# Talking-heads attention and a squared-ReLU layer on one core: the planner's DMA constants and TensorE's order replaced

## The chip, the cores and the metric

The kernel runs on one core of a Trainium2 chip. Its engines work side by side and wait for each other by semaphores: TensorE (PE, with its weight loads as PEld), VectorE (DVE), ScalarE (ACT), GpSimd (POOL) and SyncE (SP). DMA transfers are issued by POOL (queue q0) and SP (queue q1) and share 16 DMA engines. The metric is the device time of one execution in microseconds, the median of several runs.

## The reference

```python
# q, k, v: (8, 12, 448, 64); w_pre, w_post: (12, 12)
scores = scale * np.matmul(q, k.transpose(0, 1, 3, 2))
scores = np.einsum('bhij,hg->bgij', scores, w_pre)
scores = scores - np.max(scores, axis=-1, keepdims=True)
attn = np.exp(scores)
attn = attn / (np.sum(attn, axis=-1, keepdims=True) + 1e-09)
attn = np.einsum('bhij,hg->bgij', attn, w_post)
attn_out = np.matmul(attn, v)
x = attn_out.transpose(0, 2, 1, 3).reshape(3584, 768)
h = np.maximum(x @ w_in, 0.0)          # w_in (768, 2048)
out = h * h @ w_out                    # w_out (2048, 768)
```

The heads are mixed by a 12 x 12 matrix before the softmax and by another one after it.

## The kernel before

Each of the eight batches goes through the same steps, and the steps of several batches are interleaved. A step is cut into units of TensorE; a unit is a few matmuls into one or two of the eight PSUM banks, followed by evictions on ACT or DVE.

- Transposes (`emit_T`, matmuls on line 726) turn q and k into `qkt`.
- QK units (`emit_QK`, L879) multiply a tile of up to 128 query rows with all keys, for one pair of heads; the result is evicted into `stage` (L486 on ACT, L487 on DVE). `stage` holds three such tiles (NSG = 3). A unit is written as two matmuls of 128 columns, or as four of 64 where `QK_QUAD` has a "1".
- Relayouts (`emit_rel`, L925): a DMA issued by SP moves ten query rows of all 12 heads, a chunk of 105 KB, from `stage` to one of 16 slots of `dring`, where the heads lie along the partitions. A relayout waits for all evictions of its tile and for the pre unit that last read its slot.
- Pre units (`emit_pre`, L948) mix the heads of a pair of chunks; they are the only readers of `dring`. ACT takes the exponential with row sums (L965), DVE the reciprocal (L979), POOL scales the second mixing matrix (L986) and a part of the exponentials (L1001).
- The first 22 chunks of batch 0 go another way: direct units (`emit_direct`, L824) multiply with q already scaled by the mixing weights, with no relayout. The scaled q lies in the space of `w_out_sb` and `h2t` until then.
- Post units (`emit_post`, L1036 and L1050) mix the heads after the softmax and transpose on the way; their results go to `a2t` (L486, L487). AV units (`emit_AV`, L1120) multiply with v.
- First-layer units (`emit_F1`, L1176 in full tiles, L1184 in half-row tiles) and second-layer units (`emit_F2`, L1303 or L1311; L1251 for the last two tiles) are the two matrix products behind attention. ReLU is taken at the eviction (L1213, L1214), the square on DVE (L1223).
- Filler matmuls (L599) keep TensorE's array busy in the first 60 us where the planner sees a gap.

Loads of q, k, v and of both weight matrices and the stores of the output are issued by POOL. In the first 60 us that includes both weight matrices, eight loads of 384 KB each.

Nothing of the order is written out by hand except TensorE's. `_Plan.run` plays the whole program through with a cost for each task. TensorE takes its units from ten streams (transposes 0, QK 1, pre 2, post 3, AV 4, direct 5, first layer 6 and 7, second layer 8 and 9), and `ORDER` is the string that says which stream is next; within a stream units keep their order. Every other task is placed on its engine when the plan finds it ready, and evictions (`FLEX`) go to ACT or DVE, whichever the plan expects to end them earlier. So the constants of the plan and `ORDER` set the order on every engine; the waits between engines are real semaphores.

For DMAs the plan keeps two queues, "move" (relayouts) and "load" (everything else). In `dma_next` a transfer that is alone goes at full rate, and where both queues move at once each goes at a part of it. `_finish` adds `MARGIN` to the time at which a task that waits for a DMA may start, by the DMA's kind and the waiting engine: the first number up to 110 us, the second behind it.

Of the kernel before, what the change touches and what calls it, by code (L numbers as in the profile page):

```python
# [10 lines left out]
PE = "pe"  # L11
# [4 lines left out]
FLEX = "flex"  # L16
# [7 lines left out]
DMA_AHEAD = 3900.0  # L24
DMA_SLOW = {"move": 1.0, "load": 1.04}
DMA_END = {"move": 3700.0, "load": 2300.0}
MARGIN = {("move", PE): (1200.0, 700.0), ("move", FLEX): (1900.0, 1600.0),
          ("load", PE): (0.0, 900.0)}
INF = float("inf")
ORDER = (  # L30
    "0010555105055105515555551155311555513005555555315555135500155555531355331552200355511155"
    "1123333242234421126631731367227322776333631627613167122244413176313762122777623376633366"
    "2127776201902938338392281938020224441223663200811181118333813277116621277133626613377132"
    "2441141337721267612667322001667722383383338226771020283167202760238113813183138314212442"
    "2229391119333933922291444229119316116337221763363372217601026713722633602027237318302028"
    "1181118322911931393139312422442218113813381138322444221636372127633637212763362002277200"
    "2611637337339202091229119118133813181318222444223933191139331922244422818138333836212672"
    "2176336020167137336222772200637316722009119131922393831383118311822244422183138313822444"
    "2286113617137336221673373621167200227633713702206228318338382002911192229391393319222931"
    "9383138111811381224442244422367116317373337226666221763733637212791229833839228833932244"  # L40
    "42228823238687666733633637777866444776676668678676787977788999898999"
)
F1_FULL = "1111111111111111111111111111111100000000000001000000010000000110001010001111011111111111"
F2_FULL = "00000000000000000000000000101100"
QK_QUAD = "000000000001000000000000000000000000000000001000000000000000001000000000000000000000000000000000000000000000000000000000000000000000000000000000000000000000000"
POST_QUAD = "0000000000000000000000000000000000000000000000000000000000000000000000000000000000000000000000000000000000000000000000000000000000000000000000000000000000000000000000000000000001100000"


# [57 lines left out]
class _Plan:  # L106
# [89 lines left out]
    def _finish(self, t):  # L196
        t.done = True
        for s in t.succs:
            s.nwait -= 1
            spare = MARGIN.get((t.dma[0], s.engine), (0.0, 0.0)) if t.dma else (0.0, 0.0)  # L200
            s.avail = max(s.avail, t.end + SEM_LAT + spare[0 if t.end < 110e3 else 1])
# [14 lines left out]
    def dma_next(self, go=False):  # L216

        a = self.moving["move"][0] if self.moving["move"] else None
        b = self.moving["load"][0] if self.moving["load"] else None
        if a is None and b is None:  # L220
            return INF
        now = self.moved
        left = [a[1] if a else 0.0, b[1] if b else 0.0]
        while True:
            on = [x is not None and x[0] <= now for x in (a, b)]
            then = min([x[0] for x in (a, b) if x is not None and x[0] > now] + [INF])
            if not any(on):
                now = then
                continue
            rate = (1.0, 1.0)  # L230
            if all(on):
                rate = (0.22, 0.52)
                if b[2] <= 200.0:
                    rate = (47.8 / (54.0 + b[2]), 0.72)
            end = [now + left[i] / rate[i] if on[i] else INF for i in range(2)]
            first = min(end)
            to = min(first, then)
            for i in range(2):
                if on[i]:
                    left[i] -= (to - now) * rate[i]  # L240
            now = to
            if first <= then:
                x = (a, b)[end.index(first)]
                break
        if go:
            self.moved = now
            for i, y in enumerate((a, b)):
                if y is not None:
                    y[1] = left[i]
            t = x[3]  # L250
            self.moving[t.dma[0]].pop(0)
            t.end = max(t.end, now + DMA_END[t.dma[0]]
                        + (1800.0 if t.dma[0] == "load" and 20e3 < now < 45e3 else 0.0))
            self._finish(t)
        return now
# [96 lines left out]
def bass_talking_heads_attention__then__ffn_squared_relu_kernel(  # L352
# [45 lines left out]
    with ExitStack() as es:  # L398
# [460 lines left out]
        def emit_QK(b, T):  # L859
# [8 lines left out]
            for p in ((0, 3, 1, 4, 2, 5) if n == 0 else range(0, NP, IT // w)):  # L868
                g = _Group(2)

                quad = w == PJ or QK_QUAD[len(qk_units)] == "1"

# [608 lines left out]
```

## Time and profile before

| | |
|---|---|
| median of 3 runs | 521.75 us (521.67 to 521.86) |
| profiled execution | 521.25 us |
| its span, first to last instruction | 519.5 us |
| mean granted TensorE clock | 0.997 |
| busy: PE, PEld, DVE, ACT, POOL | 507.5, 320.9, 402.2, 434.2, 267.3 us |
| DMA moved | 72.32 MB, mean 139 GB/s |
| relayouts' queue q1 / loads' and stores' queue q0 | 36.86 MB / 33.83 MB |

The span is cut into windows by time: for each one the busy time of the engines, the clock that TensorE was granted (1.00 is full speed) and the busy share of the DMA engines are listed. A chain of waits follows the program back from its last instruction, at each step to what released it. In the timeline, numbers in brackets are the idle time of an engine before an instruction and what ended it. Ends of matmuls are modelled, and matmuls overlap, so how long a unit takes is read from the start of one unit to the start of the next.

### The profile page before, as it was taken

The page shows a single profiled execution, that of the slowest core. Times are in us where ns is not written, and L with a number is a line of the kernel's source. Part 1 is how long each engine was busy: PE and PEld are TensorE (multiplying, and loading weights), DVE is VectorE, ACT ScalarE, POOL GpSimd, SP SyncE. Part 2 cuts the span into 40 slices and gives each one's busy share as a digit, 9 for nine tenths or more (in the row PEclk, how much of TensorE's full clock was granted, in tenths as well). Part 3 has the DMA queues.
Part 4 walks back from the last instruction along what each step waited for, and adds up shares of the span by engine and source line. Part 5 has one row for each costly group of instructions (what it writes and reads, how often), then busy time and mean ns, then how long its engine had stood idle before and what let it go on. Part 6 is the DMA issues. An engine that isn't in the chain of part 4 may idle for free.

```text
span 519.5 us, 22375 instructions
## 1 busy us (share of the span) xinstructions
PE 507.5 (98%) x9163; PEld 320.9 (62%) x9163; DVE 402.2 (77%) x1032; ACT 434.2 (84%) x1249; POOL 267.3 (51%) x571
## 2 busy tenths in 40 slices
PE   7999998999999999999999999999999999999997
PEld 3455776667776664566556665566555665568874
DVE  8998997689988859879998879887897677855220
ACT  4989997889999988988889888888988887878531
POOL 9936665452674486434963459235664444343000
PEclk9999998999999999999999999999999999999999
DMA  8999999834896589746993679736994367551013
GB/s 114 193 229 183 217 173 185 179 101 105 151 190 149 132 174 186 153 92 151 176 182 71 144 161 188 159 86 139 171 174 107 89 142 144 106 117 33 3 34 88
DMA packets 83021, 72.32 MB, mean 139 GB/s; under 512 B 7160, under 2 KB 80424, under 8 KB 82920
## 3 DMA queue, kind: packets, MB, share of 16 engines
q0 software_dynamic: 37632, 33.83, 40.0%
q1 hardware_dynamic: 45000, 36.86, 29.0%
q8 instruction: 74, 1.21, 0.9%
q14 instruction: 27, 0.22, 0.1%
q10 hardware_dynamic: 288, 0.20, 0.1%
HBM read 47.27 MB, written 11.01 MB: 112 GB/s over the span
## 4 chain that ended last, share of the span: by engine, by line
PE 81%; ACT 7%; DVE 6%; DMA 3%; POOL 1%; issue 1%; SPq 0%; DVEq 0%; POOLq 0%
PE ps L1311 23%; PE ps L1184 12%; PE ps L1176 11%; PE ps L948 7%; PE ps L1120 6%; PE ps L1036 5%; PE ps L879 5%; PE ps L824 4%; ACT pring L965 3%; PE ps L1303 3%; DMA dring<-stage 2%; PE ps L1251 2%; DVE stage L487 2%; PE ps L726 2%; DVE a2t L487 2%; ACT stage L486 1%
## 5 line engine op out<-in xcount | busy, mean ns | idle before, releaser
L965 ACT ACTIVATE pring<-ps 128x448 bf16<-128x448 f32 x360 | 191.8, 560 | 11.8 <-PE ps L948 9.9
L986 POOL TENSOR_TENSOR wk2s<-wk2b,rinv 128x120 bf16<-128x120 bf16 (+1 forms) x179 | 71.4, 399 | 145.5 <-DVE rinv L979 144.0
L1311 PE MATMUL ps<-w_out_sb,h2t 64*128 64x384 bf16 x1472 | 134.7, 323 | 0.2 <-ACT pring L965 0.2
L487 DVE CAST a2t<-ps 128x420 bf16<-128x420 f32 (+1 forms) x205 | 123.1, 643 | 14.6 <-PE ps L1050 14.3
L487 DVE CAST stage<-ps 128x448 bf16<-128x448 f32 (+1 forms) x178 | 107.0, 616 | 10.9 <-PE ps L879 9.2
L486 ACT ACTIVATE stage<-ps 128x448 bf16<-128x448 f32 (+1 forms) x182 | 94.8, 555 | 14.8 <-PE ps L879 13.8
L486 ACT ACTIVATE a2t<-ps 128x420 bf16<-128x420 f32 (+1 forms) x163 | 96.4, 647 | 10.9 <-PE ps L1050 10.6
L1311 PEld LDWEIGHTS ps<-w_out_sb,h2t 64*128 64x128 bf16 x1472 | 68.0, 94 | 45.0 <-issue 2.6
L1184 PE MATMUL ps<-xt,w_in_sb 64*128 64x448 bf16 (+1 forms) x840 | 88.3, 347 | 0.2
L1348 POOL DMA_DIRECT2D out_dram<-osb x52 | 33.5, 650 | 95.6 <-ACT osb L486 33.7
L965 ACT ACTIVATION_READ_ACCUMULATOR pring<-ps 128x1 f32 x360 | 80.7, 224 | 0.0
L1176 PE MATMUL ps<-xt,w_in_sb 128*128 128x228 bf16 (+2 forms) x636 | 76.6, 273 | 0.0
L1223 DVE TENSOR_TENSOR h2t<-h1t 128x448 bf16<-128x448 bf16 (+2 forms) x176 | 56.1, 343 | 22.1 <-ACT h1t L1213 19.8
L1001 POOL TENSOR_TENSOR ptail<-pring,rinv 128x128 bf16<-128x128 bf16 x171 | 70.1, 410 | 0.0
L1176 PEld LDWEIGHTS ps<-xt,w_in_sb 128*128 128x128 bf16 x636 | 59.0, 99 | 13.8 <-ACT pring L965 1.8
L1036 PEld LDWEIGHTS ps<-wk2s,pring 60*128 60x128 bf16 (+1 forms) x2184 | 48.8, 94 | 23.7 <-ACT pring L965 2.4
L1213 ACT ACTIVATE h1t<-ps 128x448 bf16<-128x448 f32 (+2 forms) x104 | 44.3, 439 | 18.7 <-PE ps L1176 8.7
L948 PE MATMUL ps<-dring,wk 64*64 64x448 bf16 (+1 forms) x676 | 54.4, 364 | 3.4 <-DMA dring<-stage 1.9
L1184 PEld LDWEIGHTS ps<-xt,w_in_sb 64*128 64x128 bf16 x840 | 37.3, 94 | 32.8 <-PE ps L879 1.4
L1036 PE MATMUL ps<-wk2s,pring 60*128 60x60 bf16 (+1 forms) x2184 | 55.5, 187 | 1.2 <-issue 0.5
L979 DVE RECIPROCAL rinv<-rowsum 128x2 f32<-128x2 f32 (+1 forms) x184 | 29.0, 158 | 31.2 <-ACT pring L965 30.3
L879 PE MATMUL ps<-qkt 64*128 64x448 bf16 (+1 forms) x366 | 50.7, 353 | 0.5 <-DVE qkt L487 0.3
(62 smaller groups left out, 562.3 us busy)
## 6 DMA issues: line engine op xcount, KB each, us to landing
dring<-stage SPq DMA_DIRECT2D x309, 105.0 KB
out_dram<-osb POOLq DMA_DIRECT2D x52, 192.0 KB, 3.8
vraw<-in_v_dram POOLq DMA_DIRECT2D x48, 128.0 KB
qraw<-in_q_dram POOLq DMA_DIRECT2D x48, 112.0 KB, 4.5
kraw<-in_k_dram POOLq DMA_DIRECT2D x48, 112.0 KB, 5.4
w_in_sb<-in_moe_w_in_dram POOLq DMA_DIRECT2D x8, 384.0 KB, 17.1
w_out_sb<-in_moe_w_out_dram POOLq DMA_DIRECT2D x8, 384.0 KB, 16.2
dring<-stage SPq DMA_DIRECT2D x30, 42.0 KB
```

Of the source, the lines that this page charges most:

```text
L486: return eng.activation(o, i_, AF.Copy)
L487: return eng.tensor_copy(o, i_)
L879: r_ = eng.matmul(ps[y * v:(y + 1) * v, g.banks[x], 0:S], qkt[r0:r0 + 64, pp, 0, j0:j0 + v], qkt[r0:r0 + 64, pp, 1 + pb, :], start=True, s ...
L948: r_ = eng.matmul(ps[64 * y:64 * y + 64, gr.banks[x], 0:S], wk1[64 * x:64 * x + 64 - R0 * x, :], dring[64 * x:64 * x + 64 - R0 * x, (g0 + ...
L965: return eng.activation(pring[:, pr, 0:S], ps[:, gr.banks[x], 0:S], AF.Exp, accum_out=rowsum[:, pr, :])
L986: return eng.tensor_tensor(wk2s[:, p0:p0 + n, :], i0.to_broadcast([128, n, PR]), rinv[:, p0:p0 + n, :].to_broadcast([128, n, PR]), ALU.mult)
L1001: return eng.tensor_tensor(ptail[:, p0 // 2, :, :], pring[:, p0:p0 + 2, 0:PJ], rinv[:, p0:p0 + 2, :].to_broadcast([128, 2, PJ]), ALU.mult)
L1036: r_ = eng.matmul(ps[z * v:(z + 1) * v, gr.banks[x], o0:o0 + PR], pring[64 * x:64 * x + PR, pr + y, c:c + v], wk2s[64 * x:64 * x + PR, pr ...
L1176: r_ = eng.matmul(ps[:, gs[ph].banks[0], 0:n], w_in_sb[:, ft, t * 128:(t + 1) * 128], xt[:, ft, c0:c1], start=(ft == 0), stop=(ft == NFT - 1))
L1184: r_ = eng.matmul(ps[:, gs[0].banks[x], 0:n], w_in_sb[64 * y:64 * y + 64, ft, t * 128:(t + 1) * 128], xt[64 * y:64 * y + 64, ft, c0:c1], s ...
L1223: return eng.tensor_tensor(h2t[:, t16, o0:o0 + n], h1t[:, s, 0:n], h1t[:, s, 0:n], ALU.mult)
L1311: r_ = eng.matmul(ps[:, gs[0].banks[hh], 0:FH], h2t[64 * y:64 * y + 64, t16, col:col + 128], w_out_sb[64 * y:64 * y + 64, t16, hh * FH:(hh ...
```

## The change

Three things are replaced: the rates at which a relayout and a load move when both are under way, which now come from a table by the load's kind (97 the first weight matrix, 79 the second, 88 q and k, 60 v, 250 the output, 54 the last output pieces); the margins; and the two strings that set TensorE's order and the form of its QK units. No unit is added or removed. `F1_FULL`, `F2_FULL` and `POST_QUAD` stay.

```diff
-MARGIN = {("move", PE): (1200.0, 700.0), ("move", FLEX): (1900.0, 1600.0),
+DMA_SHARE = {97.0: (0.295, 0.75), 79.0: (0.325, 0.74), 88.0: (0.3, 0.76),
+             60.0: (0.39, 0.76), 250.0: (0.22, 0.52), 54.0: (0.44, 0.72)}
+MARGIN = {("move", PE): (0.0, 700.0), ("move", FLEX): (700.0, 1500.0),
           ("load", PE): (0.0, 900.0)}
 ORDER = (
-    "0010555105055105515555551155311555513005555555315555135500155555531355331552200355511155"
+    "0010155055051505511551555115555113553155550033555555550105555555311553332550220555315551"
...
-QK_QUAD = "000000000001000000000000000000000000000000001000000000000000001000000000000000000000000000000000000000000000000000000000000000000000000000000000000000000000000"
+QK_QUAD = "001000000001000000000000000000000000000000001001000000010000001000000000000000000000000000000000000000000000000000000000000000000000000000000000000000000000000"
...
             rate = (1.0, 1.0)
             if all(on):
-                rate = (0.22, 0.52)
-                if b[2] <= 200.0:
-                    rate = (47.8 / (54.0 + b[2]), 0.72)
+                rate = DMA_SHARE[b[2]]
```

All eleven rows of `ORDER` change; one is shown. By the formula that goes, the first rate was 0.317 for the first weight matrix (now 0.295), 0.359 for the second (0.325), 0.337 for q and k (0.3) and 0.419 for v (0.39). For a relayout the plan's margin up to 110 us falls from 1200 to 0 ns where TensorE waits for it and from 1900 to 700 ns where an eviction does.

More of the change, by code (lines that the diff above doesn't have):

```diff
@@ L30 @@
 ORDER = (
-    "0010555105055105515555551155311555513005555555315555135500155555531355331552200355511155"
[L32 to L41, printed above, removed]
+    "0010155055051505511551555115555113553155550033555555550105555555311553332550220555315551"
+    "2313332431244123622317667223677313361372267113667313242244137611376713127721266676623336"
+    "7277128310028323839139229839200223444132622008111811181338317222167663123776313673132621"
+    "4431411367217127766327621002677622383383338162267720028332677102208311813181338314212442"
+    "2229391139313933922291444229119116316337221763363372217620016733722631620027137383200281"
+    "1181118222939133911393124222441183138311831382224442216363372217633637212763362002277200"
+    "2611637337339200292219119118131813183318222444223931193139331922244422881383138336221672"
+    "1276200167337136336222772002736316720209119313922193831183138113822244422381381338224442"
+    "2816336117117336221673373621167200226731362002713783382228382002911392219139393319222931"
+    "9318338111811382224444442236171163377331722166662227637336372127922198338392298333832244"
+    "42228876323267886673363363676787774448687787766676697767689989889999"
 )
```

## The prediction

> **What bounds the kernel now.** First the page's busy shares, then the waits of TensorE, then its busy time by windows.
>
> ```profile
> PE 507.5 (98%) x9163; PEld 320.9 (62%) x9163; DVE 402.2 (77%) x1032; ACT 434.2 (84%) x1249; POOL 267.3 (51%) x571
> PE ps L948 <- DMA dring<-stage: 1.9, 1, 1.9
> PE ps L599 <- DVE osb L584: 1.5, 1, 1.5
> PE ps L1036 <- issue: 0.5, 1, 0.5
> ```
>
> TensorE is busy for 507.5 of 519.5 us, so 12 us are all that a new order of the same work can win from idle time, and 1.5 us of them lie before the first filler matmul, where the order does nothing. The longest single wait in the program is one: a pre unit (line 948) waited 1.9 us for a relayout, the DMA from `stage` to `dring`. The windows show where that is and what follows it (columns: sum, then busy time of PE, PEld, DVE, ACT, POOL, then granted clock, DMA share, GB/s).
>
> ```profile
> 40.00:60.00 20.00, 19.10 (x359) 11.74 (x356) 18.26 (x49) 19.78 (x65) 14.06 (x30) 1.00 1.07 192
> 60.00:76.00 16.00, 15.49 (x290) 12.12 (x290) 14.71 (x48) 15.92 (x49) 8.84 (x21) 1.00 1.00 185
> 78.00:80.00 2.00, 0.38 (x4) 0.16 (x4) 0.80 (x3) 1.35 (x6) 0.92 (x3) 0.87 1.15 199
> 80.00:82.00 2.00, 2.00 (x14) 1.50 (x11) 0.47 (x2) 1.16 (x4) 0.00 (x0) 0.50 1.04 193
> 82.00:84.00 2.00, 2.00 (x20) 1.63 (x17) 1.67 (x6) 0.36 (x1) 1.29 (x3) 0.78 0.78 153
> 160.00:500.00 340.00, 338.93 (x6309) 210.97 (x6297) 261.85 (x645) 290.03 (x835) 166.47 (x365) 1.00 0.62 129
> ```
>
> From 160 to 500 us TensorE idles 1.1 us in all: nothing is to be won there. Around 79 us it idles for most of a window, and afterwards its granted clock is 0.50 and 0.78 for two windows. The chain of waits through this place:
>
> ```profile
> 54.23 1.24 PE ps L1176 x12
> 60.88 1.80 PE ps L1176 x18
> 68.17 11.36 DMA dring<-stage
> 79.53 0.09 issue
> 79.62 0.59 PE ps L948 x4
> 80.21 3.76 PE ps L1176 x24
> ```
>
> The relayout is issued at 68.17 and lands at 79.53; the pre unit starts at 79.62. A first-layer unit is six matmuls of L1176: 1.24/2 = 0.62 us at full clock. The four units after the wait took 3.76 us and not 4 x 0.62 = 2.48: the slow clock cost 1.28 us. So this one place costs 1.9 + 1.3 = 3.2 us.
>
> Why is the relayout late? The relayouts' own DMA queue (q1) in the windows 20 to 40, 40 to 60, 60 to 80 and 80 to 100 us, against the pre matmuls of the same windows (four to a pair of chunks, so to two relayouts):
>
> ```profile
> dring<-stage SPq DMA_DIRECT2D x16, 105.0 KB
> ...
> q1 hardware_dynamic: 1510, 1.25, 24.1%
> ...
> q1 hardware_dynamic: 1763, 1.46, 28.2%
> ...
> q1 hardware_dynamic: 1883, 1.56, 30.4%
> ...
> q1 hardware_dynamic: 2477, 2.05, 36.2%
> ...
> 20.00:40.00 20.00, 0.00 (x0) 0.00 (x0) 1.00 1.26 222
> 40.00:60.00 20.00, 3.25 (x40) 0.99 (x40) 1.00 1.07 192
> 60.00:80.00 20.00, 2.86 (x34) 0.98 (x34) 0.99 1.03 189
> 80.00:100.00 20.00, 2.10 (x24) 0.62 (x20) 0.93 0.96 186
> ```
>
> At 105 KB (0.1075 MB) each, 11.6, 13.6, 14.5 and 19.1 relayouts are moved, while TensorE uses 0, 20, 17 and at most 12. The stock is 11.6, then 5.2, then 2.7, then about 10. The DMA engines are full (share about 1), shared with the loads of the weights, so relayouts come at a fixed rate, TensorE takes them faster, and the stock is down to what is still in flight just before 80 us. This stage is bound by relayout traffic at that point; the rest of the program is bound by TensorE's own work.
>
> **The change part by part.** It adds no work: the same 952 TensorE units run in another order. On TensorE, at the place of the wait (L948 pre, L879 QK, L1176 first layer, L1036 and L1050 post), before:
>
> ```order
> L1176 MATMUL ps<-xt,w_in_sb 128x228 x12
> L948 MATMUL ps<-dring,wk 64x448 x4
> L879 MATMUL ps<-qkt 64x448 x4
> L948 MATMUL ps<-dring,wk 64x448 x8
> L1176 MATMUL ps<-xt,w_in_sb 128x228 x24
> L948 MATMUL ps<-dring,wk 64x448 x4
> ```
>
> The unit that waits is the second half of the x8 row; the x24 behind it are the four slow units. TensorE, the same place in the change:
>
> ```order
> L1176 MATMUL ps<-xt,w_in_sb 128x228 x18
> L879 MATMUL ps<-qkt 128x448 x2
> L1036 MATMUL ps<-wk2s,pring 128x60 x12
> L1050 MATMUL ps<-wk2b,ptail 128x60 x2
> L879 MATMUL ps<-qkt 128x448 x2
> L948 MATMUL ps<-dring,wk 64x448 x4
> L1176 MATMUL ps<-xt,w_in_sb 128x228 x12
> L948 MATMUL ps<-dring,wk 64x448 x4
> L879 MATMUL ps<-qkt 64x448 x4
> L948 MATMUL ps<-dring,wk 64x448 x4
> L1176 MATMUL ps<-xt,w_in_sb 128x228 x36
> L948 MATMUL ps<-dring,wk 64x448 x4
> ```
>
> The unit that waited is now the third row of L948. Counted over the whole program, all units that stood ahead of it still do, and four more: three first-layer units (of those that ran slow) and one post unit.
>
> Step 1, the wait. Eighteen L1176 matmuls take 1.80 us (row above). A post unit:
>
> ```profile
> 60.01 0.34 PE L1036 MATMUL ps<-wk2s,pring 60*128 60x60 bf16 x12
> 60.19 0.19 PE L1050 MATMUL ps<-wk2b,ptail 60*128 60x60 bf16 x2
> 60.31 0.57 PE L948 MATMUL ps<-dring,wk 64*64 64x448 bf16 x6
> ```
>
> From its start to the next unit's it takes 60.31 - 60.01 = 0.30 us. Together 2.10 us are put ahead. Where TensorE stopped, at 79.62 - 1.91 = 77.7 us, it now has work until 79.8, and the relayout lands at 79.53 if it lands as before. The wait of 1.9 us is covered, with 0.3 us to spare: -1.9.
>
> Step 2, the clock. Without a stop the slow clock after it goes too: -1.3. The 0.5 us stop for "issue" left the clock of its window at 1.00, so short stops do not bring it on.
>
> Step 3, other pre units. Some come earlier against their relayouts: the margins that the planner kept at first for a relayout that TensorE waits for are now zero. No row shows those waits, so I bound them: below 0, above 1.9 us, the largest wait of this kind in the trace. Since the spare above is only 0.3 us and the stock is as thin for the pairs just ahead of it, I take +0.3, nearer to zero because one such wait is all that the present order has.
>
> Step 4, evictions. The units put ahead bring three eviction-and-square pairs and two post evictions forward, into windows where ACT is busy for 19.78 of 20 and 15.92 of 16 us. They do not stand between TensorE and the pre unit except through a PSUM bank. ACT and DVE idle in the stop and behind it (windows 78 to 84 above: 3.1 of 6 us for ACT), and that takes them up: 0. If they did hold a bank, the price is one eviction, about 0.6 us.
>
> Step 5, QK units in four matmuls for two. `QK_QUAD` sets six flags in place of three, so there are three more of them:
>
> ```profile
> 74.92 0.35 PE L879 MATMUL ps<-qkt 64*128 64x448 bf16 x2
> 76.89 0.38 PE L879 MATMUL ps<-qkt 64*64 64x448 bf16 x4
> 149.51 1.30 PE ps L1311 x16
> 156.58 1.41 PE ps L1311 x16
> ```
>
> Each costs 0.38 - 0.35 = 0.03 us more, 0.09 in all, and may save a change of the array's tiling, worth 0.11 us (the second-layer unit with and without one). Counted in both orders, such changes are 261 before and 260 now. Sum 0.0.
>
> Step 6, the rest of the order, which is swapped locally. From 160 to 500 us TensorE idles 1.1 us (row above), so at most that is won, and about as much may be lost: 0.
>
> Sum for the profiled execution: 521.25 (519.5 of span and 1.75 around it) - 1.9 - 1.3 + 0.3 = 518.35. The median of the runs is 521.75, 0.5 more, so the forecast is **518.9 us**, 0.55% faster.
>
> **The rivals.** (a) The wait moves but stays. Relayouts come at a fixed rate, so a TensorE that is 3.2 us ahead may run dry at a later pair and give all of it back: 521.7 us. Against it: from 80 to 100 us 19 relayouts land and 12 are used, so the stock grows there. For it: the spare of 0.3 us, which a slightly slower relayout uses up.
>
> (b) Slower. The relayouts of the third tile of query rows (the first of batch 1) wait for that tile's last QK unit. TensorE before, with its last QK units in the x6 and in half of the x4:
>
> ```order
> L879 MATMUL ps<-qkt 128x448 x6
> L824 MATMUL ps<-qkt,h2t 128x448 x6
> L879 MATMUL ps<-qkt 128x448 x4
> L948 MATMUL ps<-dring,wk 64x448 x4
> L1036 MATMUL ps<-wk2s,pring 128x60 x12
> ```
>
> and in the change, where the last of them is the L879 row:
>
> ```order
> L948 MATMUL ps<-dring,wk 64x448 x4
> L1120 MATMUL ps<-a2t,vraw 64x220 x6
> L1120 MATMUL ps<-a2t,vraw 64x110 x4
> L1120 MATMUL ps<-a2t,vraw 64x220 x6
> L1120 MATMUL ps<-a2t,vraw 64x110 x4
> L1036 MATMUL ps<-wk2s,pring 128x60 x12
> L1050 MATMUL ps<-wk2b,ptail 128x60 x2
> L879 MATMUL ps<-qkt 128x448 x2
> L948 MATMUL ps<-dring,wk 64x448 x4
> ```
>
> Three pre units, five post units, a filler and an AV unit now stand ahead of it.
>
> ```profile
> 47.21 0.55 PE L599 MATMUL ps<-osb 128*128 128x448 bf16 x2
> 48.09 0.34 PE L1036 MATMUL ps<-wk2s,pring 60*128 60x60 bf16 x12 [0.34 <-POOL ptail L1001]
> 48.30 0.33 PE L1036 MATMUL ps<-wk2s,pring 60*128 60x60 bf16 x12
> 50.50 0.57 PE L948 MATMUL ps<-dring,wk 64*64 64x448 bf16 x8
> 47.83 4.74 SPq L925 DMA_DIRECT2D dring<-stage  x5
> 51.38 1.65 PE ps L1120 x40
> ```
>
> That is 8 x 0.21 (48.30 - 48.09) + 0.88 (48.09 - 47.21) + 0.83 (half of 1.65) = 3.4 us more TensorE work ahead of it. If SP's queue runs out of relayouts there, every later pair lands up to 3.4 us later: 79.53 becomes 82.9, TensorE is there at 79.8 and stops for 3.1 us. With the clock loss scaled to it, 1.3 x 3.1/1.9 = 2.1, the sum is 518.05 + 3.1 + 2.1 + 0.5 = 523.8 us. Against it: the relayout above needed 11.36 us from issue to landing, so several stand in the queue ahead of each and cover a late one, and SP issued five in 4.74 us there without a stop, held by a slot that the pre unit at 50.50 frees and not by the QK units. It decides only from the point where the lateness is more than the queue's contents.
>
> (c) The wait goes but the slow clock stays, because it does not hang on this stop: 521.25 - 1.9 + 0.3 + 0.5 = 520.2 us. The rows speak against it: the clock is 1.00 in the windows shown ahead of the stop and 0.50 right behind it. [...]
>
> **How the numbers follow.** The forecast gets 0.52, (a) 0.15, (b) 0.25, (c) 0.08. Those of the forecast (a little of it lost to new waits) and of (c), with a fifth of (a), are faster by over 0.2% (1.04 us, about what a measurement of this kernel can tell from no change): 0.62. Most of (a) is within it: 0.15. (b) is slower: 0.23, as its mild form falls within. The range: below, the forecast without step 3's waits, with the stop for "issue" and 1.1 us of the rest gone too, 518.9 - 0.3 - 0.5 - 1.1 = 517.0; above, into (b) up to 523.4, little short of its full price. The forecast's own range is 517.0 to 520.5.
>
> **What would show it.** Right: no wait for `dring` over 0.5 us on TensorE before 100 us, a granted clock of 1.00 in all windows from 60 to 100, L1176 units at 0.62 us there. Step 2 is wrong if the clock drops with no stop of over 1 us ahead of it. Step 3 is wrong if several pre units wait for `dring` between 50 and 95 us. Rival (b) would show as a longer wait for `dring` near 80 us with fewer bytes on q1 from 40 to 60 us than 1.46 MB. The forecast fails if ACT or DVE, and not a relayout, turns up as what TensorE waits for between 40 and 80 us.

## The result and the profile after

The changed kernel runs in 519.34 us, the median of 8 runs, against 521.71 us for the kernel before on the same chips; the ratio is 0.9957, with a 95% interval of 0.9939 to 0.9975. A second measurement on another chip gave 519.01 against 521.33 us, ratio 0.9957 (0.9937 to 0.9977). The forecast was 518.9 us.

The first rows answer to the waits shown of before. Of the kernel after, TensorE's longest waits from 20 to 110 us (total, count, longest):

```profile
PE ps L1176 <- ACT a2t L486: 0.8, 1, 0.8
PE ps L1036 <- ACT h1t L1213: 0.6, 1, 0.6
PE ps L1036 <- POOL ptail L1001: 0.3, 1, 0.3
```

Its windows around the place of the old stop, with the columns of before (sum, busy PE, PEld, DVE, ACT, POOL, clock, DMA share, GB/s):

```profile
76.00:78.00 2.00, 2.00 (x33) 1.53 (x30) 1.88 (x6) 1.77 (x6) 1.25 (x3) 1.00 1.12 198
78.00:80.00 2.00, 2.00 (x26) 1.39 (x26) 2.00 (x7) 2.00 (x7) 0.00 (x0) 1.00 1.09 197
80.00:82.00 2.00, 2.00 (x27) 1.78 (x23) 1.94 (x6) 2.00 (x8) 1.88 (x4) 1.00 0.87 162
82.00:84.00 2.00, 2.00 (x21) 1.66 (x18) 1.93 (x8) 1.70 (x6) 1.70 (x6) 1.00 1.07 185
```

No wait for `dring` is left in the list, TensorE is busy throughout the windows around 79 us, and its clock is 1.00. The timeline of the kernel after at the same place, TensorE alone (start, length, what):

```profile
78.02 0.38 PE L948 MATMUL ps<-dring,wk 64*64 64x448 bf16 x4
78.35 1.34 PE L1176 MATMUL ps<-xt,w_in_sb 128*128 128x228 bf16 x12
79.62 0.38 PE L948 MATMUL ps<-dring,wk 64*64 64x448 bf16 x4
80.02 0.36 PE L948 MATMUL ps<-dring,wk 64*64 64x448 bf16 x4
80.32 3.76 PE L1176 MATMUL ps<-xt,w_in_sb 128*128 128x228 bf16 x36
```

The pre unit that stopped TensorE starts at 80.02 with no wait, and the six first-layer units behind it take 3.76 us, the time that four took before. The pre matmuls by window, of the kernel after:

```profile
60.00:80.00 20.00, 2.28 (x26) 0.70 (x28) 1.00 1.00 184
80.00:100.00 20.00, 2.83 (x33) 0.85 (x32) 1.00 0.98 185
```

TensorE takes 26 pre matmuls (6.5 pairs) from 60 to 80 us where it took 34, and makes up for it after 80 us (33 where it took 24), when more relayouts land: q1 moves 1.57 MB from 60 to 80 us and 1.95 MB from 80 to 100 us. More units stand ahead of the pre units of this place, as the forecast's step 1 had it.

This profiled execution took 520.99 us, the longest of the first 8. How far it had come can be read at the pre unit of chunks 30 and 31 of batch 1, near 105 us, where both orders have run the same units. It stands in a row of eight matmuls, with the next one. First the row of before, then of after:

```profile
106.65 0.62 PE L948 MATMUL ps<-dring,wk 64*64 64x448 bf16 x8
```

```profile
104.34 0.57 PE L948 MATMUL ps<-dring,wk 64*64 64x448 bf16 x8
```

It is 2.3 us ahead there, and the spans differ by 0.2 us only (519.5 and 519.3): this execution lost some 2 us later on. In its window of 160 to 500 us TensorE is busy for 337.17 us, in a second profile of the same program for 338.76:

```profile
160.00:500.00 340.00, 337.17 (x6250) 208.98 (x6235) 259.04 (x638) 288.03 (x830) 163.59 (x360) 1.00 0.62 128
```

```profile
160.00:500.00 340.00, 338.76 (x6246) 210.18 (x6243) 259.46 (x640) 288.66 (x833) 163.31 (x360) 1.00 0.63 129
```

### The profile page after: what moved, and what is told of

Read it like the earlier page. It is cut to its first block, busy times and chain, and to the rows that moved or that the text cites. A ratio compares the mean times of both kernels' runs of the same rounds, so it can differ in the third digit from the quotient of the medians.

```text
span 519.3 us, 22377 instructions
## 1 busy us (share of the span) xinstructions
PE 506.3 (98%) x9169; PEld 319.7 (62%) x9169; DVE 401.9 (77%) x1025; ACT 434.1 (84%) x1256; POOL 268.4 (52%) x571
## 4 chain that ended last, share of the span: by engine, by line
PE 73%; DVE 12%; ACT 8%; DMA 3%; issue 2%; POOL 2%; POOLq 0%; ACTq 0%; DVEq 0%
PE ps L1311 23%; PE ps L1184 10%; PE ps L1176 10%; PE ps L1120 6%; PE ps L948 6%; PE ps L879 5%; PE ps L1036 5%; ACT pring L965 4%; PE ps L1303 3%; DVE stage L487 3%; DVE a2t L487 2%; PE ps L1251 2%; DMA kraw<-in_k_dram 2%; DVE w_out_sb L802 2%; PE ps L726 2%; ACT stage L486 2%
## 5 line engine op out<-in xcount | busy, mean ns | idle before, releaser
L986 POOL TENSOR_TENSOR wk2s<-wk2b,rinv 128x120 bf16<-128x120 bf16 (+1 forms) x179 | 73.2, 409 | 145.7 <-DVE rinv L979 144.3
L487 DVE CAST a2t<-ps 128x420 bf16<-128x420 f32 (+1 forms) x208 | 124.8, 643 | 16.5 <-PE ps L1050 15.9
L486 ACT ACTIVATE a2t<-ps 128x420 bf16<-128x420 f32 (+1 forms) x160 | 94.9, 645 | 13.1 <-PE ps L1050 12.8
L1176 PE MATMUL ps<-xt,w_in_sb 128*128 128x228 bf16 (+2 forms) x636 | 75.0, 270 | 1.0 <-ACT a2t L486 0.8
```

Of the source, the lines that this page charges most:

```text
L486: return eng.activation(o, i_, AF.Copy)
L487: return eng.tensor_copy(o, i_)
L986: return eng.tensor_tensor(wk2s[:, p0:p0 + n, :], i0.to_broadcast([128, n, PR]), rinv[:, p0:p0 + n, :].to_broadcast([128, n, PR]), ALU.mult)
L1176: r_ = eng.matmul(ps[:, gs[ph].banks[0], 0:n], w_in_sb[:, ft, t * 128:(t + 1) * 128], xt[:, ft, c0:c1], start=(ft == 0), stop=(ft == NFT - 1))
```

## The experiments

In the labels, "the four units" are the three first-layer units and the post unit of the forecast's step 1. Where the edit is to `ORDER`, the piece that changes is shown; "..." stands for what is left out of a row or between rows. The expectations give absolute times, but a run is compared with the kernel before on its own chip: its median there is 521.33 us for `again`, `local`, `undo` and `undo_half`, 522.18 us for `head`, `tail`, `order_only` and `consts`, and 521.57 us for `section` and `early`.

**again**: the changed kernel, unedited, for a second profile.

> The changed kernel once more, for a second profile. Theory (the gain is the stop near 79 us and the half clock behind it): 519.3 us within 0.5, no wait for dring over 0.5 us before 100 us, granted clock 1.00 in all windows. Its first profile has a stop of 0.9 us for 'issue' near 205 us: if that belongs to the order it is there again at the same place, if it is chance it is gone or elsewhere and the profiled execution is near 519.3 instead of 521. Rival (the profiled execution of 521 is the typical one and the median was luck): 520.5 or more.

Measured: 519.01 us (ratio 0.9957, 0.9937 to 0.9977). The profiled execution took 518.58 us, with a span of 516.8. The stop for "issue" near 205 us, 0.9 us in the first profile, is not in this one. So it is not a property of the order, and the theory's numbers hold.

**local**: old constants, flags and order, the four units alone put ahead.

```diff
-    "...13763762122777623376633366"
+    "...13763767321772262376633366"
```

> The old constants, flags and order, with only the four units (three first-layer, one post) put ahead of the pre unit that stopped near 79 us. Theory: these four alone make the gain, the wait of 1.9 us and the 1.3 us of clock go, 521.7 - 3.2 = 518.5, not over 519.5; clock 1.00 from 76 to 90 us. Rival (the evictions of the four find ACT and DVE full, or the relayouts run dry at the next pair): a stop of 1 to 2 us comes back between 70 and 95 us and the time is 520.5 to 521.7.

Measured: 522.68 us, ratio 1.0016 (1.0001 to 1.0031). The theory falls. The rival's stop is there; the time lies 1 us above the rival's range, and no run shows why this kernel is slower than the one before. The timeline of `local`, TensorE:

```profile
78.18 1.34 PE L1176 MATMUL ps<-xt,w_in_sb 128*128 128x228 bf16 x12
79.45 0.74 PE L948 MATMUL ps<-dring,wk 64*64 64x448 bf16 x8
80.13 0.76 PE L1176 MATMUL ps<-xt,w_in_sb 128*128 128x228 bf16 x6
82.72 0.38 PE L948 MATMUL ps<-dring,wk 64*64 64x448 bf16 x4 [1.83 <-DMA dring<-stage]
```

The pre unit that waited before now goes through without a stop: it is the second half of the x8 at 79.45. One first-layer unit later comes the next pre unit, and that one waits 1.83 us: its relayout lands at 82.47, 3.0 us after the x8 started. The clock falls to 0.50 behind this stop, in the window of 84 to 86 us, as it did behind the old one. The cover was moved from one pair to the next.

**undo**: the changed kernel with the four units back behind the pre unit.

```diff
-    "...137611376713127721266676623336"
+    "...137611376112212737766676623336"
```

> The changed kernel with the same four units put back behind that pre unit. Theory: the pre unit stops TensorE for about 2 us near 77 us and the clock falls to about 0.5 behind it, 519.3 + 3.2 = 522.5, at least 521.3. Rival (the rest of the new order has brought the relayouts forward, so that nothing waits): 519.3 to 520.0.

Measured: 520.79 us, ratio to before 0.9985 (0.9967 to 1.0003): 1.8 us more than the changed kernel on the same chip (519.01), where the theory had 3.2. It lies between the ranges of the theory and of the rival. The chain of waits at the place shows the relayout's issue and landing, of `undo`:

```profile
68.63 0.06 SPq L925
68.74 9.71 DMA dring<-stage
```

It lands at 78.45, where it landed at 79.53 before, although it is issued 0.6 us later. So the stop is 1.0 us and not 1.9, and the clock stays at 1.00 behind it. Something else in the new order makes this relayout land earlier. The theory has the stop right; its length and, in this execution, the fall of the clock it has wrong.

**undo_half**: two of the four units put back.

```diff
-    "...137611376713127721266676623336"
+    "...137611376713122127766676623336"
```

> The changed kernel with two of the four units (1.2 us of work) put back behind that pre unit. Theory (the clock falls only behind a stop of some length): a stop of 0.5 to 1.0 us, the clock stays 1.00, 519.9 to 520.3. Rival (any stop for a relayout brings the half clock): 0.9 + 1.3, so 521.0 to 521.5. Second rival (relayouts land earlier under the new order, so that two units cover it): 519.3.

Measured: 520.52 us, ratio 0.9977 (0.9960 to 0.9994). TensorE idles 0.6 us between 76 and 80 us and the clock stays at 1.00; its idle time falls on several units and no wait for `dring` is listed. That is nearest to the theory's case, 0.2 us above its range. The pre unit that the stop belonged to waits 0.35 us here, for an eviction of `stage` on DVE; the profile does not tell whether a relayout or an eviction ends each of the small waits.

**head** and **tail**: the new order up to 105 us with the old one behind it, and the other way round. Both have the new constants and flags. The seam lies in the third row; of `head`, against the changed kernel, and of `tail`, against it too:

```diff
-    "7277128310028323839139229839200223444132622008111811181338317222167663123776313673132621"
+    "7277128310028323839139229839200224441223663200811181118333813277116621277133626613377132"
...
```

```diff
-    "0010155055051505511551555115555113553155550033555555550105555555311553332550220555315551"
+    "0010555105055105515555551155311555513005555555315555135500155555531355331552200355511155"
...
-    "7277128310028323839139229839200223444132622008111811181338317222167663123776313673132621"
+    "2127776201902938338392281938020223444132622008111811181338317222167663123776313673132621"
```

> The new order up to the pre unit at about 103 us (both orders have run the same units by then), the old order behind it; new constants and flags. Theory: all of the gain lies ahead of 100 us, 519.0 to 519.5. Rival (part of it comes from the later order): 520.3 or more.

> The old order up to about 103 us, the new one behind it; new constants and flags. Theory: 521.7 within 0.5, with the stop near 79 us and the half clock behind it as before. Rival (the later order gains): 520.5 or less. Rival (the later order loses what the stops of the first profile showed): 522.3 or more.

Measured: `head` 519.44 us, ratio 0.9963 (0.9944 to 0.9982); `tail` 522.38 us, ratio 1.0018 (0.9995 to 1.0042). The whole gain lies ahead of 105 us: `head` keeps it, and `tail` does not have it. Of the new order behind 105 us neither a gain nor a loss can be told. In absolute time `tail` is 0.2 us above its theory's range and just within that of the second rival (the later order loses), but the kernel before takes 522.18 us beside it, so the ratio doesn't show such a loss. The stop of `tail` is there (1.52 us), with the half clock behind it.

**order_only** and **consts**: the new order and flags with the old constants, and the old ones with the new constants. Of `consts`, against the kernel before:

```diff
-MARGIN = {("move", PE): (1200.0, 700.0), ("move", FLEX): (1900.0, 1600.0),
+MARGIN = {("move", PE): (0.0, 700.0), ("move", FLEX): (700.0, 1500.0),
...
-                rate = (0.22, 0.52)
-                if b[2] <= 200.0:
-                    rate = (47.8 / (54.0 + b[2]), 0.72)
+                rate = DMA_SHARE[b[2]]
```

> New order and flags, old constants, which now decide only how the other engines' work is ordered. Theory (TensorE's order alone makes the gain): 519.3 within 0.5. Rival (the evictions that the old margins place later hold TensorE up): 520.3 or more.

> New constants, old order and flags. Theory: 521.7 within 0.5, the stop near 79 us stays. Rival (the new constants by themselves place evictions and loads better): 520.7 or less, or the stop moves by over 1 us.

Measured: `order_only` 519.87 us, ratio 0.9963 (0.9943 to 0.9983); `consts` 522.32 us, ratio 1.0007 (0.9987 to 1.0027). Both lie 0.1 us above their theories' ranges, with the kernel before at 522.18 us. TensorE's order, with its flags, makes the gain; by themselves the constants bring nothing that can be told. In the profile of `consts` the stop is there, with this timeline of TensorE:

```profile
77.10 0.38 PE L948 MATMUL ps<-dring,wk 64*64 64x448 bf16 x4
79.53 0.38 PE L948 MATMUL ps<-dring,wk 64*64 64x448 bf16 x4 [2.04 <-DMA dring<-stage]
82.29 0.38 PE L948 MATMUL ps<-dring,wk 64*64 64x448 bf16 x4
```

and its clock does not fall, which no theory had expected (window of `consts`):

```profile
80.00:82.00 2.00, 2.00 (x22) 2.00 (x21) 0.97 (x4) 1.48 (x5) 0.75 (x3) 1.00 0.82 162
```

**section**: the old constants, flags and order, 27 units around the stop put into the new order among themselves.

```diff
-    "...13763762122777623376633366"
-    "2127776..."
+    "...13763767327721266676623336"
+    "7277123..."
```

> The old constants, flags and order, with the 27 units from the last pre unit before the stop to the third after it put into the new order among themselves, so that the same four units stand ahead of the pre unit that stopped and six first-layer units ahead of the next one. New theory (relayouts of one pair after the other land some 3 us apart here, so each of these pre units needs its own cover): no stop over 0.7 us between 70 and 95 us, 518.5 to 519.7. Rival (the earlier part of the new order is needed too, since it brings relayouts forward by about 1 us): stops of 0.5 to 1.5 us remain there, 520.3 to 521.5.

Measured: 521.62 us, ratio 0.9991 (0.9972 to 1.0011): no gain that can be told. The profiled execution took 520.37 us, one of the shorter ones (they run from 520.3 to 523.1), and there the longest wait of TensorE for `dring` is 0.5 us, near 70 us. A later pre unit waits 1.1 us for an eviction, in the timeline of `section`:

```profile
89.72 0.38 PE L948 MATMUL ps<-dring,wk 64*64 64x448 bf16 x4 [1.09 <-DVE a2t L487]
```

So the stop near 79 us can be covered within the old order, but the theory's "no stop over 0.7 us" fails, and over its executions the kernel is no faster. The rival's stop is there, with another cause than it named, and the time is 0.1 us above its range. Four of the 12 executions have a mean clock of 0.997 and the other eight 0.999 or 1.000, so some still lose the clock; the eight are no faster than those of before that kept it (521.0 us on the mean for both). Why they are not is open.

**early**: the new order up to about 60 us, where both have run the same units, the old one behind it; new constants and flags. Of the second row, against the changed kernel (the rows behind it are the old ones):

```diff
-    "2313332431244123622317667223677313361372267113667313242244137611376713127721266676623336"
+    "2313332431244123622317667223677313361372267113613167122244413176313762122777623376633366"
...
```

> The new order up to about 60 us (both orders have run the same units by then), the old one behind it; new constants and flags. New theory: the stop stays at the same pre unit, about as long as before (1.2 to 2.2 us), 521.0 to 522.5. Rival (the earlier part makes the relayouts land earlier and so gains by itself): the stop is 1.2 us or less, 520.5 or less.

Measured: 519.69 us, ratio 0.9967 (0.9946 to 0.9988). The rival holds: the first 60 us of the new order make most of the gain by themselves, although the old order still stops at the same pre unit. The chain of `early`:

```profile
68.60 0.25 SPq L925
68.90 9.32 DMA dring<-stage
```

and TensorE in its timeline:

```profile
77.11 0.38 PE L948 MATMUL ps<-dring,wk 64*64 64x448 bf16 x4
78.27 0.38 PE L948 MATMUL ps<-dring,wk 64*64 64x448 bf16 x4 [0.78 <-DMA dring<-stage]
81.15 0.38 PE L948 MATMUL ps<-dring,wk 64*64 64x448 bf16 x4
```

The relayout is issued 0.7 us later than before and lands at 78.22, 1.3 us earlier; the stop is 0.78 us, with the clock at 1.00 behind it. The pre unit ahead of the stop starts at 77.11, and in the timeline of before at 77.33:

```profile
77.33 0.38 PE L948 MATMUL ps<-dring,wk 64*64 64x448 bf16 x4
```

So TensorE is only 0.2 us ahead when it comes to the stop. The next pre unit starts at 81.15 and in the profile of before at 83.91, 2.8 us later. In these two profiles the gain is made at the stop and behind it, and not on the way to it.

**before_again** and **consts_again**: one more profile of each.

> The kernel before once more, for a second profile of the stop. If the half clock hangs on the stop's length alone, the stop of about 2 us is followed by it again. If it hangs on where the stop falls in time as well, it may be missing, with the stop as long as in the first profile.

> New constants with the old order once more. Its first profile has a stop of 2.0 us with no fall of the clock. If that is fixed by the program, the clock stays at 1.00 behind the stop again; if it is chance, it may fall to 0.5 this time with a stop of the same length, at the same place.

Measured, one execution each: 525.11 and 524.02 us. The stop is 2.30 and 2.27 us long. The timeline of `consts_again`, and its window behind the stop:

```profile
79.58 0.38 PE L948 MATMUL ps<-dring,wk 64*64 64x448 bf16 x4 [2.27 <-DMA dring<-stage]
84.00 0.38 PE L948 MATMUL ps<-dring,wk 64*64 64x448 bf16 x4
```

```profile
80.00:82.00 2.00, 2.00 (x13) 1.64 (x13) 0.75 (x3) 1.16 (x4) 0.31 (x2) 0.57 0.78 155
```

The same program that kept its clock in one execution lost it in another: chance, in the terms of its expectation. From the stop to the next pre unit it takes 84.00 - 79.58 = 4.42 us with the clock lost and 82.29 - 79.53 = 2.76 us with the clock kept, so the loss cost 1.7 us.

The granted clock on record for every execution says how often this happens. Of the 14 profiled executions, the five with the half clock behind a stop have a mean clock of 0.995 to 0.997 over the whole run, the others 0.999 or 1.000. In the runs of the kernel before beside these experiments, 50 of 91 executions lie at 0.995 to 0.997 and the rest at 0.999 or 1.000; of the 18 executions of the changed kernel (first measurement and `again`) none lies below 0.999. At 0.997 or less lie, of 12 executions each, none of `undo_half`, one of `early`, `head` and `order_only`, two of `undo`, four of `local` and `section`, seven of `tail` and `consts`. The mean does not say where in a run the clock was low.

## Why the prediction was right

The forecast was 0.4 us below the result, with the right place and the right sign. That it came so near is in part luck: the four units of step 1 alone bring nothing (`local`), the cover needed an earlier landing and six more units that the sum left out, and the clock's 1.3 us were counted as if every execution lost them. Point by point:

- What bounds the kernel: right. All of the gain is ahead of 105 us (`head`, `tail`). At the pre unit near 105 us the profiles that run the old order up to there stand at 106.65 (before), 109.06 (before_again), 106.69 and 108.23 (`consts`, twice) and 107.41 (`tail`), 107.6 on the mean; those with the new order at 104.34 and 104.27 (after, twice), 104.10 (`head`) and 105.21 (`order_only`), 104.5 on the mean. The 3.1 us between them stand beside the forecast's 3.2 - 0.3. The medians differ by 2.3 us: the profiled executions with the old order are a few, four of the five lost their clock, and two were long ones. (The forecast's 952 units are 948 in the strings of both kernels; nothing hangs on that.)
- Step 1, the wait: its size was near and the reason given for it was not whole. Of the executions beside `again`, those of before that kept their clock take 520.8 us on the mean, the changed kernel 519.5: 1.3 us without the clock, where steps 1 and 3 make 1.6. "The wait of 1.9 us is covered, with 0.3 us to spare" counted the four units ahead of one pre unit. `local` has just these four, and the stop only moves to the next pre unit. The new order covers that one too, by the six units of the x36 row, which the forecast's own fence showed and its sum left out. And "if it lands as before" failed to the good side: with the new order's first 60 us the relayout lands 1.1 to 1.3 us earlier (`undo`, `early`). The fixed rate of relayouts that the forecast reasons with is not in its own rows of q1 either, which go from 1.25 to 2.05 MB in 20 us. `early` alone gains 1.9 us against the kernel before on its chip, where the whole change gains 2.3 on another.
- Step 2, the clock: the loss of 1.3 us was real in the profile shown and is gone, but it belongs to that execution and not to every one of the program (`consts` twice). It counts in full in a sum made against that profile, and in part in the medians. Beside `again` 17 of 33 executions of before lost it; they take 522.2 us on the mean and the other 16 520.8, so over all executions the loss is worth about 0.7 us there, half of the 1.3.
- Step 3, new waits: put at +0.3. None for `dring` appears in the list of after from 20 to 110 us. Waits of 0.8 and 0.6 us for ACT, which the first profile has ahead of 76 us, are not in the second one. By the forecast's own sign of failing (ACT, and not a relayout, as what TensorE waits for between 40 and 80 us) the first profile speaks against it; but the waits belong to that execution and not to the order.
- Step 4, evictions: no stop for a bank of over 0.8 us was seen in the kernel after. In `section`, a pre unit waited 1.1 us for an `a2t` eviction, so this cover is thin too.
- Step 5, the flags, was not tried by itself; `tail` has all six with the old order ahead of 105 us and is no faster.
- Step 6, the rest of the order: right, nothing that can be told (`tail`, 1.0018 with 1.0 in its interval).
- Rival (a), the wait that moves to the next pair, is what `local` did: the same edit as step 1 without the rest. The forecast held the growing stock from 80 to 100 us against it; that sum over 20 us hid that the next relayout is still 3 us away.
- Rival (b) came true in its first half only: fewer relayouts move from 40 to 60 us, 1.33 MB against the 1.46 that it named, and the one of the stop is issued 0.6 to 0.7 us later (`undo`, `early`). But it lands over 1 us earlier, and no longer wait follows. The queue of the kernel after from 40 to 60 us:

```profile
q1 hardware_dynamic: 1605, 1.33, 25.9%
```

From issue to landing this relayout takes 9.3 to 12.1 us (`early`, `consts`), so the time of its issue alone does not set its landing.
- Rival (c), that the clock stays slow without the stop, did not happen: the granted clock of the kernel after is 1.00 in the windows of 60 to 80 and 80 to 100 us.

What is open: why the relayouts land earlier with the new first 60 us. The bytes of the two queues from 60 to 78 us, first of before, then of `early` (packets, MB, share):

```profile
q0 software_dynamic: 2573, 1.90, 69.6%
q1 hardware_dynamic: 1692, 1.40, 30.5%
```

```profile
q0 software_dynamic: 2482, 1.83, 70.0%
q1 hardware_dynamic: 1715, 1.42, 30.6%
```

The relayouts moved are nearly the same; the loads are 0.07 MB fewer in that stretch and 0.10 MB more ahead of 60 us (5.56 against 5.46 MB from 20 to 60 us). Other profiles go with these two: q0 moves 5.46 to 5.48 MB from 20 to 60 us where the old order runs first (before, `consts`, `section`) and 5.54 to 5.60 MB where the new one does (the kernel after twice, `undo`, `early`), although one load of the second weight matrix fewer is issued there (7 and not 8). That loads moved while fewer relayouts did, and so left the DMA engines freer later, would fit with this, but is not shown: the shares of the two queues from 60 to 78 us differ by 0.4 and 0.1 points in the rows above, and no run holds it by itself.

## What to carry to other kernels

Where transfers land one behind the other at intervals, here some 3 us (`local`), covering one stop can uncover the next: count the work between each consumer and the next against the interval of arrival, not the cover of the first one alone. Before a late transfer's landing is taken as fixed, look at the order of the work well ahead of it: that of the first 60 us moved it by 1.1 to 1.3 us here (`undo`, `early`); by what means is open. And make a second profile of the same program before a loss in the first one is put into a sum.

## What the runs showed of the hardware

The fall of TensorE's clock behind a stop is not fixed by the program. Stops for a relayout of 1.9 (before), 2.30 (before_again), 2.27 (`consts_again`), 1.83 (`local`) and 1.52 us (`tail`) were followed by a granted clock of 0.50 to 0.57 in a window of 2 us; behind one of 2.04 us (`consts`) it stayed at 1.00, and so it did behind those of 1.0 us (`undo`) and 0.78 us (`early`). The window of `tail` behind its stop:

```profile
82.00:84.00 2.00, 2.00 (x13) 1.58 (x12) 0.60 (x3) 0.36 (x1) 1.59 (x4) 0.50 0.78 154
```

How long a stop must be for this is not shown: the stop of 2.04 us that kept its clock is longer than three that lost it (1.52, 1.83 and 1.9 us).
